# The filter rows of a long convolution at other distances in the DRAM scratch

## The chip, the cores and the metric

The kernel runs on one core of one Trainium2 chip. A core has a matrix engine (TensorE, PE in the profile), a vector engine (VectorE, DVE), a scalar engine (ScalarE, ACT), a general engine (GpSimd, POOL) and a sync engine (SyncE, SP) that here does nothing but issue DMA transfers. Sixteen DMA engines move data between DRAM and the on-chip memory SBUF. Matrix products land in a second on-chip memory, PSUM, of eight banks. Each engine runs its own list of instructions in order, and semaphores make one wait for another. The metric is the device time of one execution, in microseconds (us).

## The reference

Two independent computations are put side by side in the output, 512 columns each.

```python
def _A_ref(x, wqkv, wo):                      # attention: S = 2048, D = 512, 32 heads of 16
    qkv = transpose((x @ wqkv).reshape(B, S, 3, H, Dh), 2, 0, 3, 1, 4)
    q, k, v = qkv[0], qkv[1], qkv[2]
    scores = einsum("bhqd,bhkd->bhqk", q, k) * (Dh ** -0.5)
    p = softmax(scores, axis=-1)
    o = einsum("bhqk,bhkd->bhqd", p, v)
    return transpose(o, 0, 2, 1, 3).reshape(B, S, D) @ wo

def _B_ref(q, k, v, shift_k, ssm_k, ssm_D):   # gated long convolution, 512 channels
    k_shift = sum over t of k_pad[:, t:t + S, :] * shift_k[:, 3 - t]
    kv = k_shift * v
    y = causal convolution of kv with ssm_k along S   # written with FFTs
    y = y + kv * ssm_D
    return q * y

return concatenate([_A_ref(...), _B_ref(...)], axis=-1)
```

Inputs and output are bf16.

## The kernel before

Attention. The scores of 2048 queries by 2048 keys for 32 heads are made in blocks of 128 keys by 512 queries, and each block becomes one PSUM bank of 128x512. Two or three blocks form a chunk (T in the code). For each chunk TensorE makes the scores (line 791), ScalarE takes the exponentials of two banks at once (line 798, tile PT), VectorE and GpSimd take those of a third block by a polynomial (lines 817, 826, 827 and 290), and TensorE multiplies the results with the values (line 866). ScalarE thus has one instruction per chunk, 726 in all, each over 128x1024 elements.

Convolution. It runs on TensorE between the chunks, channel by channel, as products with Toeplitz matrices. For channel row d a tile of WR holds, in partition p, the 2048 filter values that begin p elements later than those of partition 0. One DMA per channel row builds it: its source is one row of the DRAM tensor `kz_scratch`, read 128 times, each time 2 bytes further (line 977). That is 128 reads of 4096 bytes out of one run of some 4.35 KB, 512 KB in all. WR has 14 such buffers (R_W = 14). Four channel rows are a quad, and the 64 small matmuls of a quad (line 998, in `conv_lags`) read their four buffers in turn. When a quad's last matmul has ended, four buffers are free, and SyncE issues the loads of the rows that lie 14 further on (`load_wr`, line 972, called from `conv_lags`). There are 512 such loads, in the order of d.

The scratch is written once, early. `kz_turn` (line 627) reverses the filter into KZS, a part of the WR buffers, with VectorE: partition p holds the four channels 4p to 4p+3, each as 2048 values and 128 zeros, 2176 elements or 4352 bytes. `kz_store` (line 632) adds the direct term ssm_D and issues four stores on SyncE's queue, one for each of the four channels of a partition. Each store takes one row of 4352 bytes from each of the 128 partitions. The rows are not stored in channel order: channel `chan(d)` lies in row d, so that the four channel rows of a quad are right for the four column strips of TensorE. In the scratch before, row d begins at byte 4352 d.

What stands behind the stores in SyncE's queue. `kz_store` is called together with `load_kv(5, ...)`: SyncE then issues the load of a piece of v (into QN) and of a piece of k (into QT), and GpSimd issues three more loads of k. VectorE multiplies these with the taps of the short filter (`kv_chunk`, lines 598, 602 and 618), pieces j = 7, 6, 5, ... 0 in that order, into KVP, the other operand of the convolution. When a piece is done, the loads of a later piece and some of the first loads of filter rows are issued, in the same queue of SyncE. The first 14 filter loads wait for all the stores (`h_kzw[0]`); later ones wait only for TensorE. The convolution begins when piece 0 is done (`start_conv`).

Order. The lists of PE, ACT, DVE and POOL are laid out beforehand by a planner in the kernel's code, which estimates when each operation ends (the class `Eng`, `Job` queues with due times). The planner takes 5600 ns for the four loads of a quad (DMA_NS), and SyncE's issues cost it nothing. The chip only runs the finished lists.

Of the kernel before, what the change touches and what calls it, by code (L numbers as in the profile page):

```python
# [7 lines left out]
BF16 = mybir.dt.bfloat16  # L8
# [4 lines left out]
S = 2048  # L13
# [11 lines left out]
C = 512  # L25
NB = S // 128
PAD = 128
LKZ = PAD + S
R_W = 14
R_PT = 5  # L30
R_O = 8
# [140 lines left out]
def bass_concat_heads__mha_block__ssm_conv_h3__prompt_kernel(  # L172
# [10 lines left out]
    out: bass.AP,  # L183
):
    x2, q2, k2, v2, out2 = A_x[0], B_q[0], B_k[0], B_v[0], out[0]
    kz_ap = nc.dram_tensor("kz_scratch", (C, LKZ), BF16).ap()

    ctxs = []

# [4 lines left out]
    def sem(name):  # L194
        return enter(nc.semaphore(name))

    def sb(name, shape, dt=BF16):
        return enter(nc.sbuf_tensor(name, shape, dt))
# [6 lines left out]
    PT = sb("PT", [128, R_PT, 3 * QB])  # L205
    WR = sb("WR", [128, R_W, S])
    KVP = sb("KVP", [128, 4 * NB + C * NB])
# [20 lines left out]
    def xn(t):  # L228
# [6 lines left out]
    wr_flat = WR[:, :, :].rearrange("p r w -> p (r w)")  # L235
    KZS = wr_flat[:, 0:4 * LKZ].rearrange("p (c m) -> p c m", c=4)
    DSS = wr_flat[:, 4 * LKZ:4 * LKZ + 4].rearrange("p (c m) -> p c m", m=1)
    o1 = 5 * S
# [10 lines left out]
    pe, act, dve, pool, sp = [Eng(sem(n), *k) for n, k in (("s_pe", (170.0,)), ("s_act", (100.0,)), ("s_dve", (-10.0, -85.0)),  # L249
                                                           ("s_pool", ()), ("s_sp", ()))]  # L250
# [93 lines left out]
    def dve_op(fn, deps=(), cost=692.0):  # L344
        return dve.op(fn, [force(d) for d in deps], cost=cost)
# [16 lines left out]
    def dma(eng, dsem, outp, inp, deps=(), transpose=False):  # L362
        h = dsem.add()

        def fn(e):
            f = e.dma_start_transpose if transpose else e.dma_start
            f(outp, inp).then_inc(dsem.sem, 16)  # L367
        eng.op(fn, deps, inc=False)
        return h
# [5 lines left out]
    d_tap, d_kz, d_kzw, d_wo = [DmaSem(sem(n)) for n in ("d_tap", "d_kz", "d_kzw", "d_wo")]  # L375
# [3 lines left out]
    d_outA = [DmaSem(sem(f"d_outA{i}")) for i in range(R_A)]  # L379
    d_wr = [DmaSem(sem(f"d_wr{i}")) for i in range(R_W)]  # L380

# [82 lines left out]
    h_kz0 = pool.op(lambda e: e.memset(KZS[:, :, S:S + PAD], 0.0))  # L464
# [127 lines left out]
    def kv_chunk(j):  # L592
        b = kvbuf[kv_buf[j]]
        st = {}

        def tap(m):
            in1 = TB[:, m:m + 1, :].broadcast_to([128, 2, D])
            st[m] = dve_job(lambda e: e.tensor_tensor(b[m], b[m], in1, ALU.mult),
                            [h_kv[(j, 0)], h_kv[(j, 1)], h_tb[m]], 750.0, 3000.0)

        def add(m):
            st["a"] = dve_job(lambda e: e.tensor_tensor(b[3], b[3], b[m], ALU.add), [st[m], st[3], st.get("a")], 750.0, 3500.0)

        def last():
            def then(h):
                h_kvfree[j] = h
                nxt = {4: 1, 3: None, 2: 0}.get(j, j - 3)
                if nxt is not None and nxt >= 0:
                    load_kv(nxt)
                for d in {6: (0, 1), 5: (2, 3), 4: (4, 11), 3: (8, 9, 12, 13), 1: (5, 6, 7)}.get(j, ()):  # L610
                    load_wr(d, [h])
                if j == 5:
                    load_qn(0, [h_kzt[0]], 4, NB)
                    line[0] += 5000.0
                elif j == 0:
                    start_conv(h)
            for i in range(2):
                dve_job(lambda e, i=i: e.tensor_tensor(KV[:, :, NB - 1 - 2 * j - i, :], quads(b[3][:, i, :]), quads(b[4][:, i, :]), ALU.mult),  # L618
                        [st["a"], h_xt[0]], 460.0, 4000.0 + i, then if i else None)
        return [lambda m=m: tap(m) for m in (3, 2)] + [lambda: add(2), lambda: tap(1), lambda: add(1),  # L620
                                                       lambda: tap(0), lambda: add(0), last]

    h_kzw = [None]
# [7 lines left out]

    def kz_store():
        h = dve_op(lambda e: e.tensor_tensor(KZS[:, :, S - 1:S], KZS[:, :, S - 1:S], DSS, ALU.add), [h_kzt[0]], 100.0)
        rows = kz_ap.rearrange("(o e h j) m -> o h e j m", e=2, h=2, j=2)
        for i in range(4):
            h_kzw[0] = dma(sp, d_kzw, rows[:, :, 1 - i % 2, i // 2, :], KZS[:, i, :], [h, h_kz0])

    kv_pieces += [lambda c=c: kz_turn(c) for c in range(4)] + [lambda: (kz_store(), load_kv(5, h_kzt[0]))]
    for j in range(7, -1, -1):
        kv_pieces += kv_chunk(j)  # L640
# [28 lines left out]
    def turn_first(cs, t0, dep):  # L669
        def fn(e):  # L670
            ins = None
            for c in cs:
                for t in range(t0, t0 + 2):
                    pbf = PS[:, first_bank[c], :].bitcast(BF16)
                    ins = e.transpose(pbf[:, 128 * t:128 * t + 128],
                                      xn(t)[:, 128 * c:128 * c + 128], IDN[:, :])
            return ins
        return pe_op(fn, [dep, h_idn], full(128, 2 * len(cs)))
# [3 lines left out]
    for c in range(4):  # L682
        h = turn_first([c], 2, h_xn[0])
        src = PS[:, first_bank[c], :].bitcast(BF16)[:, 0:512]
# [8 lines left out]
    def first_q(dc):  # L693
        return pe_op(lambda e: e.matmul(PS[:, 6, :], lhsT=WQ[:, dc, 0:128], rhs=xT[:, dc, 0:512],
                                        start=(dc == 0), stop=(dc == 3)), [h_x[0][dc], h_wq[0]], full(512, 1))

    def first_k(bank, c0, c1):
        def fn(e):
            ins = None
            for dc in range(4):  # L700
                ins = e.matmul(PS[:, bank, c0:c1], lhsT=WK[:, dc, 0:128], rhs=xT[:, dc, c0:c1],
                               start=(dc == 0), stop=(dc == 3))
            return ins
        return pe_op(fn, [*h_x[0], h_wk[0], bank_free[bank]], full(c1 - c0, 4))

    for dc in range(4):
        h = first_q(dc)
    evac_unit(("q", 0, 0), 6, h)
    h = first_k(7, 0, 128)
# [223 lines left out]
    def op_mm(qb, t, j0, j1, bank):  # L933
        dd = [bank_free[bank] if j0 == 0 else None, h_wop[0]]
        dd += [h_otn.get((4 * qb + j, t + 1), h_otn[4 * qb + j]) for j in range(j0, j1)]

        def fn(e):
            ins = None
            for j in range(j0, j1):
                ins = e.matmul(PS[:, bank, :], lhsT=OTN[:, (4 * qb + j) % R_O, t * 128:(t + 1) * 128], rhs=WOP[:, j, :],  # L940
                               start=(j == 0), stop=(j == 3))
            return ins
        return pe_op(fn, dd, full(512, j1 - j0))
# [28 lines left out]
    def load_wr(d, deps=()):  # L972
        r = d % R_W
        deps = [h_kzw[0], *deps] if d < R_W else [h_wrfree[d - R_W]]
        if d < R_W:
            line[0] += 1350.0
        src = bass.AP(tensor=kz_ap.tensor, offset=kz_ap[d, 0].offset, ap=[[1, 128], [1, S]])
        h_wr[d] = dma(sp, d_wr[r], WR[:, r, :], src, deps)

    def load_qn(i, deps, t0, t1):  # L980
# [3 lines left out]
    def conv_lags(qd, n0, n1):  # L984
# [6 lines left out]
        def fn(e):  # L991
            ins = None
            for n in range(n0, n1):
                for c in range(4):
# [4 lines left out]
                                   lhsT=KVP[:, o:o + 4 * (m * NB - n) - 3:4],  # L999
                                   rhs=WR[:, d % R_W, 128 * (NB - 1 - n):128 * (NB - n)],  # L1000
                                   start=(n == 0), stop=(n == NB - 1), tile_position=(0, 32 * c))
            return ins
        h = pe_op(fn, deps, [("col", c, 128) for n in range(n0, n1) for c in range(4)])
        if n1 == NB:
            for c in range(4):
                h_wrfree[4 * qd + c] = h
                if 4 * qd + c + R_W < C:
                    load_wr(4 * qd + c + R_W)
            if qd % 8 == 7:
                half = qd // 8 % 2  # L1010
                src = PS[:, BGB, :]
                src = bass.AP(tensor=src.tensor, offset=PS[:, BGB, 127:128].offset,
                              ap=[src.ap[0], [128, 4], [-1, 128]])
                bank_free[BGB] = dve_job(lambda e: e.tensor_copy(YB[:, half, :].rearrange("p (k i) -> p k i", k=4), src),
                                         [h, (lambda: h_yb.get(qd // 8 - 2, WAIT)) if qd >= 16 else None])
                h_yb_in[qd // 8] = bank_free[BGB]
# [39 lines left out]
    def start_conv(h):  # L1056
        h_kvc[0] = h
        state["started"] = True
        load_wr(10, [h])
        load_qn(0, [h], 0, 4)  # L1060
        now = at_of(h)
        state["dma"] = max(line[0], now) + 5000.0
        state["wr"] += [now - 1000.0, max(line[0], now) + 2000.0, state["dma"] - 1400.0]
        state["dma"] -= 1400.0
# [281 lines left out]
    for t in range(4):  # L1346
        h = op_mm(qb, t, 3, 4, tail_banks[t])
# [55 lines left out]
```

## Time and profile before

| | |
|---|---|
| Median of 3 runs | 846.76 us (844.92 to 847.79) |
| The profiled execution | 848.2 us, with a span of 846.4 us from its first to its last instruction |
| ScalarE (ACT) | busy 819.2 us, 97% |
| VectorE (DVE) | busy 798.4 us, 94% |
| TensorE (PE) | busy 719.9 us, 85%; granted clock 0.989 in the mean |
| GpSimd (POOL) | busy 290.6 us, 34% |
| DMA | 295.69 MB, 349 GB/s over the span |

How to read it. A row of the groups has line, engine, operation, out<-in tiles, shapes and count, then the busy time and the mean duration of one, then the idle time of the engine ahead of them and what ended most of it. "idle before <-X" says that X released the wait; "issue" is a wait for nothing that the profile shows. A row of stretches gives, for each window of the span, the busy time of each engine with the number of its instructions, the granted clock of TensorE, the mean busy share of the 16 DMA engines and what they moved per second. A row of the timeline gives a start, a duration (from the first start to the last end, where several are merged), engine, line, operation and count. SPq is SyncE's queue: the time shown there is that of issuing a transfer, not of moving the data, and "DMA to landing" is the time from the start of an issue until all of its data has arrived.

### The profile page before, as it was taken

What the parts mean: (1) busy time and instruction counts of PE and PEld (TensorE: products, weight loads), DVE (VectorE), ACT (ScalarE), POOL (GpSimd) and SP (SyncE); (2) the same over time, 40 slices, a digit from 0 to 9 for tenths busy, and PEclk for the clock granted to TensorE, in tenths of its full rate; (3) what the DMA queues carried; (4) which work ended last, traced back from release to release, by engine and by line L of the source; (5) the groups of instructions that cost most, each with busy time, mean ns of one, the idle gap of its engine ahead of it and who ended that gap; (6) DMA issues with size and microseconds to landing.
All of it is one profiled execution on the core that took longest, in us unless ns stands there. A gap on an engine that the chain in (4) does not pass through costs nothing.

```text
span 846.4 us, 29917 instructions
## 1 busy us (share of the span) xinstructions
PE 719.9 (85%) x13144; PEld 310.1 (37%) x13144; DVE 798.4 (94%) x1346; ACT 819.2 (97%) x732; POOL 290.6 (34%) x323
## 2 busy tenths in 40 slices
PE   8999888888888888888888888888888988888897
PEld 3322333433343343333333333333333343333332
DVE  3998899999999999999999899999999999999996
ACT  6998999999999999999999899999999999999997
POOL 3232233334333333333333433333332334333431
PEclk9999999999999999999999999999999999999999
DMA  9878699999999999999998999999999999999810
GB/s 325 302 266 291 219 405 351 382 407 406 387 351 389 387 408 382 386 359 389 386 381 303 374 365 407 366 409 377 359 343 363 374 411 384 380 395 387 342 51 26
DMA packets 88867, 295.69 MB, mean 349 GB/s; under 512 B 11173, under 2 KB 19362, under 8 KB 88482
## 3 DMA queue, kind: packets, MB, share of 16 engines
q1 hardware_dynamic: 82818, 280.00, 87.5%
q0 software_dynamic: 3776, 12.58, 4.2%
q8 instruction: 105, 1.72, 0.8%
q10 hardware_dynamic: 2144, 1.18, 0.5%
q14 instruction: 24, 0.20, 0.1%
HBM read 287.31 MB, written 6.42 MB: 347 GB/s over the span
## 4 chain that ended last, share of the span: by engine, by line
ACT 71%; PE 13%; DVE 12%; issue 2%; DMA 1%; POOL 1%; ACTq 0%; DVEq 0%
ACT PT L798 71%; PE PS L791 5%; PE PS L866 2%; DVE PTD L827 2%; DVE EM L826 2%; DVE EI L817 2%; PE PS L521 2%; DVE WKV L826 2%; PE PS L998 1%; PE PS L940 1%; DMA WKV<-in_A_wqkv_dram 1%; DVE OUTA L952 1%; PE PS L507 1%; PE PS L514 1%; DMA QT<-in_B_k_dram 1%
## 5 line engine op out<-in xcount | busy, mean ns | idle before, releaser
L798 ACT ACTIVATE PT<-PS 128x1024 bf16<-128x1024 f32 (+1 forms) x726 | 815.6, 1328 | 16.4 <-PE PS L791 14.8
L791 PE MATMUL PS<-QT,KTo 32*128 32x512 bf16 x2048 | 287.4, 387 | 113.3 <-ACT PT L798 92.8
L998 PE MATMUL PS<-WR,KVP 128*30 128x128 bf16 (+15 forms) x8192 | 258.7, 222 | 4.7 <-issue 4.2
L998 PEld LDWEIGHTS PS<-WR,KVP 128*29 128x29 bf16 (+15 forms) x8192 | 178.2, 95 | 79.7 <-issue 40.4
L290 POOL TENSOR_SCALAR EM<-EI 128x512 f32<-128x512 uint16 x131 | 126.9, 969 | 224.3 <-DVE WKV L826 114.8
L290 POOL TENSOR_SCALAR WKV<-EI 128x512 f32<-128x512 uint16 x130 | 125.9, 969 | 208.8 <-DVE EM L826 100.3
L866 PE MATMUL PS<-PT,VAF 128*32 128x512 bf16 x1787 | 188.6, 394 | 1.8 <-issue 0.7
L817 DVE TENSOR_SCALAR EI<-PS 128x512 int32<-128x512 f32 x261 | 177.3, 679 | 7.0 <-PE PS L791 6.7
L826 DVE SCALAR_TENSOR_TENSOR EM<-EM 128x512 f32<-128x512 f32 x262 | 175.0, 683 | 2.3 <-POOL EM L290 2.0
L826 DVE SCALAR_TENSOR_TENSOR WKV<-WKV 128x512 f32<-128x512 f32 x260 | 173.1, 682 | 2.0 <-POOL WKV L290 1.8
L791 PEld LDWEIGHTS PS<-QT,KTo 32*128 32x128 bf16 x2048 | 71.8, 91 | 275.3 <-ACT PT L798 218.2
L827 DVE SCALAR_TENSOR_TENSOR PTD<-EI,EM 128x512 uint16<-128x512 int32 x131 | 89.1, 681 | 0.4
L827 DVE SCALAR_TENSOR_TENSOR PTD<-EI,WKV 128x512 uint16<-128x512 int32 x130 | 88.2, 679 | 0.3
L866 PEld LDWEIGHTS PS<-PT,VAF 128*32 128x32 bf16 x1787 | 47.4, 93 | 109.1 <-issue 99.0
L866 PE MATMUL PS<-PTD,VAF 128*32 128x512 bf16 x261 | 79.2, 394 | 0.3
L1120 PE MATMUL PS<-IDN,ZER 128*32 128x512 bf16 x396 | 44.1, 382 | 0.0
L892 DVE STREAM_TRANSPOSE DT<-PS 128x512 f32<-128x512 f32 x31 | 22.1, 712 | 8.4 <-PE PS L866 8.2
L866 PEld LDWEIGHTS PS<-PTD,VAF 128*32 128x32 bf16 x261 | 19.8, 95 | 19.6 <-issue 8.1
L542 DVE TENSOR_TENSOR QT<-PS,MSK 128x1024 bf16<-128x1024 f32 x15 | 18.3, 1222 | 4.0 <-PE PS L507 3.9
L521 PE MATMUL PS<-WKV,xT 128*128 128x512 bf16 x64 | 19.2, 384 | 0.1
L367 POOL DMA_DIRECT2D out_dram<-OUTA x12 | 7.1, 593 | 34.8 <-DVE OUTA L952 34.8
L367 POOL DMA_DIRECT2D WR<-in_B_k_dram x15 | 11.0, 737 | 22.8 <-DVE KVP L618 14.8
(80 smaller groups left out, 295.2 us busy)
## 6 DMA issues: line engine op xcount, KB each, us to landing
WR<-kz_scratch SPq DMA_DIRECT2D x512, 512.0 KB, 8.0
WR<-in_B_k_dram POOLq DMA_DIRECT2D x15, 256.0 KB, 7.4
kz_scratch<-WR SPq DMA_DIRECT2D x4, 544.0 KB, 6.6
out_dram<-QN POOLq DMA_DIRECT2D x2, 1024.0 KB, 7.9
QT<-in_B_k_dram POOLq DMA_DIRECT2D x7, 256.0 KB, 6.2
out_dram<-OUTA POOLq DMA_DIRECT2D x12, 128.0 KB, 5.7
WR<-in_B_v_dram SPq DMA_DIRECT2D x5, 256.0 KB, 8.5
WR<-in_B_k_dram SPq DMA_DIRECT2D x5, 256.0 KB, 10.4
```

The costliest lines, as they stand in the source:

```text
L290: q.h = pool.op(lambda e: e.tensor_scalar(UB[m % len(UB)], f, PA, PB, ALU.mult, ALU.add), [h, fx.h, free], cost=Beside((h[0], h[1] + 1)))
L521: return e.matmul(PS[:, bank, :], lhsT=xT[:, dc, kt * 128:(kt + 1) * 128], rhs=WV[:, dc, :], start=(dc == 0), stop=(dc == 3))
L542: hh = dve_job(lambda e: e.tensor_tensor(QT[:, qb % 2, 2 * o:2 * o + 2, :], src, MSK[:, :, 0:1].broadcast_to([128, 2, QB]), ALU.mult), [h, ...
L791: ins = e.matmul(PS[:, bank, :], lhsT=KTo[32 * s:32 * s + 32, g // 2, kt * 128:(kt + 1) * 128], rhs=QT[32 * s:32 * s + 32, qb % 2, g, :], ...
L798: h_exp[T] = act.op(lambda e: e.activation(PT[:, T % R_PT, 0:n * QB], PS[:, banks[0]:banks[0] + n, :].rearrange("p b f -> p (b f)"), ACT.E ...
L817: h_fix[i] = job(lambda e: e.tensor_scalar(ei, PS[:, bank, :], FIX_LO, FIX_ADD, ALU.max, ALU.add), [h, h_pair.get(i - 4)], 692.0, end)
L826: js.append(job(lambda e, c=c: e.scalar_tensor_tensor(u, u, c, u, ALU.add, ALU.mult), [js[-1]], 693.0, due + 700.0 * (len(js) - 3)))
L827: js.append(job(lambda e: e.scalar_tensor_tensor(PTD[:, i % 4, :].bitcast(UINT16), ei, 2.0 ** -9, u, ALU.mult, ALU.add), [js[2], (lambda: ...
L866: ins = e.matmul(PS[32 * s:32 * s + 32, pvb(qb * NG + g), :], lhsT=VAF[:, kt, h * VW:h * VW + 32], rhs=rhs, start=first[b], stop=last[b], ...
L892: h_t = dve_job(lambda e: e.transpose(out=dt, in_=PS[:, pvb(n), :]), [h, h_mult.get(n - 2 if n == 2 else n - 1) if n != 1 else None], 717. ...
L998: ins = e.matmul(PS[32 * c:32 * c + m * NB - n, BGB, 128 * kk:128 * kk + 128], lhsT=KVP[:, o:o + 4 * (m * NB - n) - 3:4], rhs=WR[:, d % R_ ...
L1120: ins = e.matmul(PS[32 * s:32 * s + 32, pvb(n), :], lhsT=ZER[:, 0:32], rhs=IDN[:, :].rearrange("p (a f) -> p a f", a=1).broadcast_to([128, ...
```

## The change

The scratch becomes a flat tensor. Its 512 rows form four quarters of 128, and in each quarter the rows lie at another distance: 4480 bytes for rows 0 to 127, 5120 for 128 to 255, 6400 for 256 to 383 and 8448 for 384 to 511 (PITCH counts elements of 2 bytes). A list `kz_at` holds each row's first element. A row itself stays as it was, 2176 elements.

Since one store's rows no longer lie at one distance over the whole tensor, each of the four stores is cut into four, one for each quarter: 16 stores of 32 partitions in place of 4 of 128. Quarter g lies in partitions 32g to 32g+31. A load reads the same row as before, from its new place. In the lists of instructions, the four `kz_scratch<-WR` of SyncE become 16 at the same place; those of the other engines, and SyncE's other transfers and waits, stand in the same order as before.

```diff
+PITCH = (2240, 2560, 3200, 4224)
...
-    kz_ap = nc.dram_tensor("kz_scratch", (C, LKZ), BF16).ap()
+    kz_ap = nc.dram_tensor("kz_scratch", (C // 4 * sum(PITCH),), BF16).ap()
+    kz_at = [C // 4 * sum(PITCH[:d // 128]) + d % 128 * PITCH[d // 128] for d in range(C)]
...
         h = dve_op(lambda e: e.tensor_tensor(KZS[:, :, S - 1:S], KZS[:, :, S - 1:S], DSS, ALU.add), [h_kzt[0]], 100.0)
-        rows = kz_ap.rearrange("(o e h j) m -> o h e j m", e=2, h=2, j=2)
-        for i in range(4):
-            h_kzw[0] = dma(sp, d_kzw, rows[:, :, 1 - i % 2, i // 2, :], KZS[:, i, :], [h, h_kz0])
+        for g in range(4):
+            for i in range(4):
+                dst = bass.AP(tensor=kz_ap.tensor, offset=kz_at[128 * g + 4 * (1 - i % 2) + i // 2],
+                              ap=[[8 * PITCH[g], 16], [2 * PITCH[g], 2], [1, LKZ]])
+                h_kzw[0] = dma(sp, d_kzw, dst, KZS[32 * g:32 * g + 32, i, :], [h, h_kz0])
...
-        src = bass.AP(tensor=kz_ap.tensor, offset=kz_ap[d, 0].offset, ap=[[1, 128], [1, S]])
+        src = bass.AP(tensor=kz_ap.tensor, offset=kz_at[d], ap=[[1, 128], [1, S]])
```

## The prediction

> **What bounds the kernel now.** I read the page first: the busy times, then the chain of waits, then the groups on that chain and the DMA issues.
>
> ```profile
> span 846.4 us, 29917 instructions
> PE 719.9 (85%) x13144; PEld 310.1 (37%) x13144; DVE 798.4 (94%) x1346; ACT 819.2 (97%) x732; POOL 290.6 (34%) x323
> ...
> ACT 71%; PE 13%; DVE 12%; issue 2%; DMA 1%; POOL 1%; ACTq 0%; DVEq 0%
> ...
> L798 ACT ACTIVATE PT<-PS 128x1024 bf16<-128x1024 f32 (+1 forms) x726 | 815.6, 1328 | 16.4 <-PE PS L791 14.8
> ...
> L998 PE MATMUL PS<-WR,KVP 128*30 128x128 bf16 (+15 forms) x8192 | 258.7, 222 | 4.7 <-issue 4.2
> ...
> WR<-kz_scratch SPq DMA_DIRECT2D x512, 512.0 KB, 8.0
> ...
> kz_scratch<-WR SPq DMA_DIRECT2D x4, 544.0 KB, 6.6
> ```
>
> ScalarE sets the end: its 726 exponentials fill 815.6 of 846.4 us and stand idle for 16.4. DMA has 1% of the chain. The change touches two groups only, the 512 loads of filter rows and the four stores behind them, so the question is what either keeps waiting. The instructions of line 998 read the loaded rows; for them I asked who ended their waits, and for SyncE's queue what its issues wait for.
>
> ```profile
> L998 PE MATMUL PS<-WR,KVP x8192: 216/219/314, 90.9 to 812.8; 128*20 128x128 bf16 x9, 128*18 128x128 bf16 x9, 128*22 128x128 bf16 x8, 128*13 128x128 bf16 x8
> ...
>   issue: 44.6, 160
>   DVE YB L1014: 0.3, 1
> ```
>
> ```profile
> SPq L367 <- PE PS L998: 311.7, 86, 13.1
> ```
>
> No wait of line 998 was ended by a DMA. It is the other way round: SyncE waits 311.7 us for line 998 to free the buffers. How much time the data has in hand shows in one typical quad, number 100. Its last two loads were issued at 648.3 and 648.6 (first block: the issues, then their time to landing), its first matmul started at 658.92 (second block).
>
> ```profile
> L367 SPq DMA_DIRECT2D WR<-kz_scratch x2: 320/376/433, 648.3 to 648.6; - x2
> ...
> DMA to landing us min/median/max: 4.8/5.8/6.7
> ```
>
> ```profile
> 658.92 0.26 PE L998 MATMUL PS<-WR,KVP 128*32 128x128 bf16 x4
> ```
>
> The later one landed at 648.6 + 6.7 = 655.3, 3.6 us ahead of its use. That is the slack of the filter loads.
>
> It is a narrow one. The 128 quads take 812.8 - 90.9 = 721.9 us, 5.64 us each, and a quad needs 4 x 512 KB = 2.097 MB: the convolution asks for 372 GB/s. What the DMA engines can give shows where they were behind and worked without a gap, from 182 to 207.5 us:
>
> ```profile
> DMA  9999999999999999999999999999999999999999
> ...
> DMA packets 2826, 10.35 MB, mean 406 GB/s; under 512 B 313, under 2 KB 313, under 8 KB 2820
> ```
>
> At 406 GB/s a quad takes 5.17 us. So the reserve is 0.47 us per quad, 8% of the rate.
>
> **The change part by part.** The sum is made against the profiled execution: span 846.4, 848.2 us in all, so 1.8 us lie around the span. The median of the runs shown, 846.76, is 1.4 below it; I carry the difference over to the median.
>
> *1. The 512 loads from new places.* Number, size and order stay, and each still reads one run of some 4.35 KB 128 times, shifted by 2 bytes. Only the place of the next row differs. Before, 10.35 MB at 406 GB/s are some 20 consecutive rows, lying over 87 KB of the scratch at 4352 bytes, with no slice of that window under 90% busy; none of these places was slower than the others. I take 0 for this part. Upwards, the nearest rows are stretches in which the DMA engines gave less:
>
> ```profile
> 90.00:130.00 40.00, 33.90 (x707) 15.13 (x706) 36.62 (x61) 39.65 (x36) 14.66 (x15) 1.00 0.88 331
> ...
> 610.00:650.00 40.00, 33.08 (x676) 15.12 (x677) 37.46 (x64) 38.05 (x34) 12.68 (x14) 0.96 0.98 359
> ```
>
> These are no measured limits, but nothing nearer exists. At 359 GB/s a quad takes 5.84 us, 0.20 too long; over the 32 quads of a quarter 6.4 us, less 3.6 in hand, +2.8. At 331 it is 6.34 us, 0.70 too long, 22.4 less 3.6, +18.8. Downwards: all idle time of PE ahead of line 998 is 4.7 us, and if every part of it were hidden waiting for rows, faster loads could win no more: -4.7. I choose 0 because the window at 406 GB/s is the same operation at full load. What covers these loads is the 3.6 us and the 8%; when both are gone, line 998 waits in PE's list, behind it the next scores (line 791), and ScalarE behind those.
>
> *2. Sixteen issues for four.* SyncE's list around the stores:
>
> ```profile
> 26.60 4.00 SPq L367 DMA_DIRECT2D kz_scratch<-WR  x4
> 30.64 1.29 SPq L367 DMA_DIRECT2D QN<-in_B_v_dram  x1
> 31.98 1.58 SPq L367 DMA_DIRECT2D QT<-in_B_k_dram  x1
> 34.59 0.42 SPq L367 DMA_DIRECT2D WR<-in_B_v_dram  x1
> 35.05 0.58 SPq L367 DMA_DIRECT2D WR<-in_B_k_dram  x1
> 42.53 0.37 SPq L367 DMA_DIRECT2D WR<-in_B_v_dram  x1
> ...
> 43.46 0.94 SPq L367 DMA_DIRECT2D WR<-kz_scratch  x2
> ```
>
> Four issues took 4.00 us. An issue of 32 partitions is in no row. The lower bound is the shortest issue of a whole filter load above, 0.32 us: 16 x 0.32 = 5.1, 1.1 longer than now. The upper bound is the mean of today's stores, 1.0 us: 16.0, 12 longer. I take the 0.43 us of an unhindered filter load, the nearest kind: 6.9 us, +2.9. Queued behind are the v and k loads of piece 5, then those of piece 4. The k of piece 5 is needed first:
>
> ```profile
> DMA to landing us min/median/max: 7.6/7.6/7.6
> ```
>
> ```profile
> DMA to landing us min/median/max: 2.9/8.0/14.1
> ```
>
> ```profile
> 43.02 1.28 DVE L598 TENSOR_TENSOR QT<-QT,WR 128x1024 bf16<-128x1024 bf16 x2
> ```
>
> The first row is that load's time to landing, the second that of all transfers into or out of WR, the third the load's first use in VectorE's list. It was issued at 31.98, landed at 39.6 and was used at 43.02: 3.4 us in hand. They cover the +2.9 even if it were passed on whole. At +12 the load would be issued at 44 and land, with the shortest landing of 2.9 us, at 46.9: VectorE would stand 3.9 us. I count 0 here.
>
> *3. The stores' own transfer.* The bytes stay (4 x 544 KB = 2.23 MB), but each store now draws on 32 partitions. While the old stores ran, the DMA engines were full:
>
> ```profile
> 30.00:34.00 4.00, 4.00 (x36) 1.62 (x36) 3.96 (x8) 4.00 (x5) 0.00 (x0) 1.00 1.00 382
> ```
>
> At 382 GB/s the stores take 5.8 us. If 32 partitions give the same rate, this part costs 0; if a quarter of the partitions gave half of it, 5.8 us more, and the k of piece 5 would land at 45.4 instead of 39.6: VectorE stands 45.4 - 43.02 = 2.4 us. Of that the end can take all or nothing. The chain of waits in order of time says how it would get there:
>
> ```profile
> 73.05 0.43 DVE KVP L618
> 73.54 2.66 POOL QT L424
> 76.48 2.39 POOL QT L367 x4
> 78.88 4.35 DMA QT<-in_B_k_dram
> 83.25 0.69 DVE QT L598
> ```
>
> Here VectorE's work on the pieces is itself on the chain, up to the last piece's loads; a delay at 43 that is not made good by 73 arrives at the end. I take +0.5 for parts 2 and 3 together (bounds 0 and 3.9), nearer to 0, because the 3.4 us in hand are used up only when the stores take 5.8 + 3.4 = 9.2 us, at a rate under 241 GB/s.
>
> The Trainium skill speaks against that choice: "SBUF — State Buffer", section "Door 1: The DMA port swizzle", says that a transfer over 32 partitions reaches 8 of the 16 DMA ports, and gives 189 GB/s against 328 for 128 partitions. By these figures the stores would take, as an estimate, 10.1 us, the k of piece 5 would land at 43.9, and the sum would hold up to 0.9 instead of 0.5; no row here shows a 32-partition transfer.
>
> *4. The first filter loads wait for the stores.* They are issued from 43.46 on, when VectorE has freed the queue. The stores:
>
> ```profile
> L367 SPq DMA_DIRECT2D kz_scratch<-WR x4: 603/825/1617, 26.6 to 29.0; - x4
> ...
> DMA to landing us min/median/max: 4.7/6.6/8.2
> ```
>
> The last one landed at 29.0 + 8.2 = 37.2 at the latest. Delayed by 5.8 it lands at 43.0: nothing. The lists of the other engines are unchanged.
>
> Sum: 0 + 0 + 0.5 + 0 = +0.5; 848.7 in the profiled terms, **847.3 us** against the median of 846.76.
>
> **The rivals.**
>
> *A quarter of the rows is slow (slower).* One of the distances sets consecutive rows so that the DMA engines get less than 372 GB/s from them. Place: PE ahead of line 998, in one quarter of the time from 91 to 813 us. It decides from 8% loss on, after the 3.6 us are used up. Price +2.8 to +18.8, the middle +10: **857 us**. For it: the reserve is small, and the stretches above dip to 331. Against it: 406 GB/s over 20 rows at 4352 bytes. [...]
>
> *The stores from 32 partitions are half as fast.* Part 3 in full: VectorE stands 2.4 us ahead of 43 to 45 us and passes all of it on: **849.2 us**. For it: VectorE's pieces lie on the chain. Against it: between 43 and 73 us VectorE has idle time that may take it up:
>
> ```profile
> 53.00:63.00 10.00, 8.94 (x56) 2.25 (x54) 8.79 (x15) 9.95 (x12) 4.25 (x6) 1.00 0.92 301
> ```
>
> VectorE is busy 8.79 of 10 us there.
>
> *The loads get faster, and it counts.* Other distances lift the dips, and the 4.7 us ahead of line 998 fall away: **842.1 us**. Against it: with 3.6 us in hand nothing waits for the rows; a faster load waits longer in its buffer.
>
> *The change does nothing at all* is within my forecast: 846.8.
>
> **How the numbers follow.** About 0.3% (2.5 us) is what a measurement of this kernel can tell from no change: faster means below 844.2, slower above 849.3. Chances: forecast 0.50, a slow quarter 0.23, slow stores 0.17, faster loads 0.10. The forecast's own range is 845 to 849.3, with 0.03 of it above; slow stores fall 0.07 above, where the issues' upper bound adds to them. Slower: 0.23 + 0.07 + 0.03 = 0.33. Faster: 0.10. The same: 0.57. The range goes down to 844.0, leaving out most of the faster case, and up to 854, where half of the slow-quarter case, some 0.11, is left out.
>
> **What would show it.** Right: line 998 has no wait that a DMA ended, the filter loads land in 8.0 us in the median in all four quarters (used from 91 us on in steps of 180.5, issued some 20 us, 14 rows, ahead of that), the 16 stores are issued in about 7 us, and the first L598 on QT at 43 us has no idle time ahead of it. Slow stores: that L598 starts at 45 with a wait ended by a DMA. A slow quarter: landing times well over 8 us in one quarter with a DMA share at 1.00 and under 372 GB/s, and idle time ahead of L998. My forecast is wrong if ScalarE's idle time (16.4 us) grows by more than 2.5 us.

## The result, and the profile after

| | before | after |
|---|---|---|
| Median | 847.27 us (844.92 to 851.16, 4 runs) | 867.9 us (866.78 to 871.03, 4 runs) |
| Ratio of the times | | 1.0263, 95% interval 1.0231 to 1.0294 |
| Profiled execution | 848.2 us, span 846.4 us | 867.73 us, span 866.0 us |
| ScalarE busy, idle ahead of its exponentials | 819.2, 16.4 us | 821.3, 34.0 us |

The changed kernel is 2.6% slower, and the prediction of no change was wrong. (Two of the 24 executions behind e4_odd_shift below were slow ones of some 865 us and are left out of its medians; the one of them with a trace lost its time ahead of the convolution, which began at 104.8 instead of some 91 us, and had no wait of line 1002 for a load, so the loss shown here is another one.) In the code after, the line numbers have moved: 791 has become 795, 798 is 802, 998 is 1002, 367 is 369, 598 is 600. From the page of after, the span, the GB/s of 40 equal slices (each 21.65 us), the chain of waits, the two groups on it and the two groups of transfers that the change touches:

```profile
span 866.0 us, 29883 instructions
...
GB/s 326 273 284 287 227 399 360 386 406 402 362 383 386 392 408 364 401 372 398 379 387 291 362 411 385 382 402 365 337 317 318 344 344 334 346 354 342 351 66 25
...
ACT 50%; DVE 18%; DMA 16%; PE 11%; SPq 2%; issue 2%; POOL 1%; ACTq 0%; DVEq 0%
...
L802 ACT ACTIVATE PT<-PS 128x1024 bf16<-128x1024 f32 (+1 forms) x726 | 817.7, 1314 | 34.0 <-PE PS L795 32.0
...
L1002 PE MATMUL PS<-WR,KVP 128*30 128x128 bf16 (+15 forms) x8192 | 261.3, 224 | 22.8 <-DMA WR<-kz_scratch 20.0
...
WR<-kz_scratch SPq DMA_DIRECT2D x512, 512.0 KB, 8.6
...
kz_scratch<-WR SPq DMA_DIRECT2D x16, 136.0 KB, 3.8
```

DMA had 1% of the chain and now has 16%; ScalarE's share has fallen from 71% to 50%. The matmuls on the filter rows stood idle for 4.7 us, none of it for a DMA; now it is 22.8 us, 20.0 of them for the loads. ScalarE's idle time has grown by 17.6 us and its busy time by 2.1 us, together 19.7 against a span that is 19.6 us longer: nine tenths of the loss is ScalarE standing idle, nearly all of it for scores (line 795: 32.0 us where line 791 had 14.8), which stand behind line 1002 in PE's list.

Where in the span it happens, the GB/s row already tells: from the 29th slice on (606 us) only two slices reach 350, where most of the earlier ones are above 360. By stretches, with the columns that the prediction used (the last three are granted clock, DMA share, GB/s), first around that point:

```profile
570.00:610.00 40.00, 33.62 (x682) 14.97 (x687) 38.31 (x64) 38.87 (x34) 14.23 (x15) 0.96 1.02 375
610.00:650.00 40.00, 31.55 (x647) 14.14 (x640) 37.69 (x65) 38.27 (x34) 13.04 (x14) 1.00 1.01 326
```

The prediction placed the loads of a quarter 20 us ahead of a use in steps of 180.5 us from 91 us: the last quarter's loads, rows 384 to 511 at 8448 bytes, begin at about 612 us. There the DMA engines remain as busy as in the stretch ahead (1.01) and move 13% less. (The kernel before has a dip of its own in this stretch, to 359.) One stretch inside each quarter, after:

```profile
110.00:270.00 160.00, 135.40 (x2750) 62.09 (x2761) 157.03 (x264) 158.69 (x140) 56.48 (x62) 1.00 1.01 387
290.00:430.00 140.00, 115.02 (x2463) 53.45 (x2462) 138.58 (x236) 139.98 (x123) 51.19 (x52) 1.00 1.02 387
470.00:590.00 120.00, 99.65 (x2065) 45.74 (x2068) 116.67 (x196) 117.58 (x104) 42.92 (x44) 0.99 1.01 388
650.00:800.00 150.00, 118.40 (x2305) 52.27 (x2315) 129.38 (x216) 132.21 (x114) 47.04 (x50) 0.94 0.99 339
```

and the last of them before:

```profile
650.00:800.00 150.00, 126.12 (x2609) 57.15 (x2605) 147.18 (x249) 148.82 (x131) 54.53 (x58) 0.99 1.01 385
```

Three quarters move 387 to 388 GB/s; the fourth gets 339, where the convolution asks for 372 and the same stretch had 385. The time of a load from issue to landing (minimum, median, maximum) in the last quarter says the same; after:

```profile
DMA to landing us min/median/max: 8.8/13.9/18.2
```

before:

```profile
DMA to landing us min/median/max: 4.8/7.9/10.7
```

Loads that landed 3.6 us ahead of their use now take 6 us longer. The chain of waits in order of time, after (start, duration, what), shows what became of it:

```profile
689.85 5.06 ACT PT L802 x4
697.08 13.47 DMA WR<-kz_scratch
710.69 0.53 PE PS L1002 x24
...
714.45 16.67 DMA WR<-kz_scratch
731.26 0.66 PE PS L1002 x20
731.92 0.54 PE PS L795 x3
...
734.78 18.62 ACT PT L802 x16
...
759.49 13.27 DMA WR<-kz_scratch
```

Before, the chain from 689.66 us on was ScalarE's exponentials one after the other:

```profile
689.66 81.44 ACT PT L798 x71
```

Now loads stand on it again and again, with pieces of PE, VectorE and ScalarE between: of the chain from 690 to 830 us the loads are 51.3% and the exponentials 16.9%. The end of it, from the instructions of line 1002 (count, shortest, median and longest in ns, first and last start):

```profile
L1002 PE MATMUL PS<-WR,KVP x8192: 216/219/314, 91.7 to 832.4; 128*5 128x128 bf16 x9, 128*20 128x128 bf16 x9, 128*18 128x128 bf16 x9, 128*22 128x128 bf16 x8
```

The convolution takes 740.7 us instead of 721.9, +18.8, and starts 0.8 later; together that is the 19.6 of the span.

### The profile page after: what moved, and what is told of

Its sections match the earlier page's. It is cut to its first block, busy times and chain, and to the rows that moved or that the text cites. A ratio compares the mean times of both kernels' runs of the same rounds, so it can differ in the third digit from the quotient of the medians.

```text
span 866.0 us, 29883 instructions
## 1 busy us (share of the span) xinstructions
PE 720.5 (83%) x13098; PEld 310.7 (36%) x13144; DVE 799.7 (92%) x1346; ACT 821.3 (95%) x732; POOL 291.3 (34%) x323
## 4 chain that ended last, share of the span: by engine, by line
ACT 50%; DVE 18%; DMA 16%; PE 11%; SPq 2%; issue 2%; POOL 1%; ACTq 0%; DVEq 0%
ACT PT L802 50%; DMA WR<-kz_scratch 13%; PE PS L795 4%; DVE PTD L831 3%; DVE EI L821 3%; DVE EM L830 3%; DVE WKV L830 3%; SPq L369 2%; PE PS L870 2%; PE PS L1002 2%; DMA WR<-in_B_ssm_D_dram 2%; DMA QT<-in_B_k_dram 1%; DVE QT L544 1%; PE PS L509 1%; DVE DT L896 1%
## 5 line engine op out<-in xcount | busy, mean ns | idle before, releaser
L1002 PE MATMUL PS<-WR,KVP 128*30 128x128 bf16 (+15 forms) x8192 | 261.3, 224 | 22.8 <-DMA WR<-kz_scratch 20.0
L870 PEld LDWEIGHTS PS<-PTD,VAF 128*32 128x32 bf16 x261 | 19.8, 95 | 20.3 <-issue 9.0
```

What stands on the lines that cost most here:

```text
L870: ins = e.matmul(PS[32 * s:32 * s + 32, pvb(qb * NG + g), :], lhsT=VAF[:, kt, h * VW:h * VW + 32], rhs=rhs, start=first[b], stop=last[b], ...
L1002: ins = e.matmul(PS[32 * c:32 * c + m * NB - n, BGB, 128 * kk:128 * kk + 128], lhsT=KVP[:, o:o + 4 * (m * NB - n) - 3:4], rhs=WR[:, d % R_ ...
```

## The experiments

Two questions were open: is it the place of the rows and not the sixteen stores, and what about 8448 bytes is bad. The first kernel measures loads by themselves. Every time stands beside runs of the kernel before from the same chip; m1_rates and e1 to e3 ran on one chip, m2_rates, m3_rates, e4 and e5 on a second, m4_steps, e6 and e7 on a third, so rates of different kernels may also differ by the chip.

### Eight distances, loads alone (m1_rates)

```diff
+PITCH = (4352, 8448, 12544, 8192, 16640, 6400, 10240, 4352)
...
+            for s, p in enumerate(PITCH):
+                for d in range(N):
...
+                    src = bass.AP(tensor=rows[s].tensor, offset=d * p // 2, ap=[[1, 128], [1, S]])
+                    e.dma_start(WR[:, r, :], src).then_inc(d_wr[r], 16)
```

> All computation is left out: the kernel writes zeros to the output and then only loads filter-like rows, 64 at each of eight distances in turn, 14 loads in flight, nothing waiting for TensorE. The distances are, in this order, 4352, 8448, 12544, 8192, 16640, 6400, 10240 and again 4352 bytes. Theory A (what counts is the distance's remainder modulo 8192: consecutive rows that begin at nearly the same remainder crowd one part of the memory): 1.25 to 1.30 us per load at 4352, 12544 (the same remainder, 4352) and 6400; 1.5 to 1.6 us at 8448 and 16640 (both remainder 256) and as much or more at 8192 (remainder 0); 10240 (remainder 2048) in between. Theory B (a longer distance is slower as such): 4352 and 6400 at 1.27, 8448 at 1.55, and 12544 and 16640 at 1.55 or more. Theory C (the distance does not count; the last quarter is slow for another reason): 1.25 to 1.30 us at all.

Each distance has 64 loads of 512 KB, one distance after the other. The stretches in which only loads of one distance ran (columns here: window, length, DVE, POOL, clock, DMA share, GB/s), for 4352, 8448, 12544 and 8192:

```profile
115.00:180.00 65.00, 0.00 (x0) 0.00 (x0) 1.00 1.03 410
190.00:280.00 90.00, 0.00 (x0) 0.00 (x0) 1.00 0.96 330
295.00:360.00 65.00, 0.00 (x0) 0.00 (x0) 1.00 1.03 410
375.00:470.00 95.00, 0.00 (x0) 0.00 (x0) 1.00 1.01 313
```

16640 gave 359; 6400, 10240 and the second 4352 gave 410. For a load of 524,288 bytes, 410 GB/s are 1.28 us, 359 are 1.46, 330 are 1.59 and 313 are 1.68. A longer distance is not slower as such (12544 is as fast as 4352), and no other transfer runs beside these loads, so the slow rates need no other traffic. The remainder 2048 (10240), expected in between, was as fast as the rest. Slow are the distances that are a multiple of 8192 or 256 more.

### Sixteen stores, old distance (e1_all4352)

```diff
-PITCH = (2240, 2560, 3200, 4224)
+PITCH = (2176, 2176, 2176, 2176)
```

> The 16 stores of the changed kernel, but all rows 4352 bytes apart, as before the change. If the loss of 20 us lies in the distances (A and B): 847 us, within 0.3% of before (ratio 0.997 to 1.003), and no wait of line 1002 that a DMA ended. If the 16 smaller stores cost what I had allowed them: +0.5 to +2.4 us. If the last quarter is slow for another reason than distances (C): 866 us as in the changed kernel.

847.62 us (843.39 to 850.82, 10 runs) against 845.58 for the kernel before (15 runs); ratio 1.0017, interval 0.9989 to 1.0045. The row of the matmuls:

```profile
L1002 PE MATMUL PS<-WR,KVP 128*30 128x128 bf16 (+15 forms) x8192 | 259.4, 222 | 8.0 <-issue 6.7
```

The row names only what ended most of the 8.0 us; among the rest is a single wait for a load, of 0.5 us, where none was expected. Cutting the stores costs nothing that can be measured, though up to 0.45% (3.8 us) is inside the interval; the loss of 20 us comes with the distances.

### The slow quarter moved to the front (e2_first8448)

```diff
-PITCH = (2240, 2560, 3200, 4224)
+PITCH = (4224, 2560, 3200, 2240)
```

> The distances 8448 and 4480 bytes change places: 8448 in the first quarter, 4480 in the last. A and B: the stretch from 110 to 270 us moves about 335 GB/s with the DMA engines fully busy and line 1002 waits for DMAs there, the stretch from 650 to 800 us moves 375 to 390 GB/s with no such wait; in all some 862 to 870 us, since the slack is the same there. C: the last quarter stays slow, and the first stays at 370 to 400 GB/s.

875.52 us, one run. First and last quarter by stretches:

```profile
110.00:270.00 160.00, 129.84 (x2353) 55.68 (x2357) 134.02 (x223) 136.65 (x118) 47.27 (x49) 0.88 0.98 322
...
650.00:800.00 150.00, 126.60 (x2636) 57.88 (x2633) 147.38 (x248) 149.47 (x132) 53.23 (x57) 1.00 1.01 387
```

The slow stretch goes where the 8448 bytes go, and the last quarter, now at 4480, is as it was. So it is neither the end of the span nor the end of the tensor. The loss is 29.9 us, larger than expected: the rate in the first quarter is lower (322 against 339), and the granted clock is 0.88 against 0.94. Why the same distance costs more there isn't settled; the waits of line 1002 for loads are no longer in sum than in the changed kernel (19.8 us against 20.0).

### The last quarter at 12544 (e3_last12544)

```diff
-PITCH = (2240, 2560, 3200, 4224)
+PITCH = (2240, 2560, 3200, 6272)
```

> The last quarter at 12544 bytes instead of 8448. A (remainder 4352 modulo 8192, that of the kernel before): 847 us, ratio to before 0.997 to 1.004, no wait of line 1002 that a DMA ended. B (longer is slower): 866 us or more.

849.26 us (844.05 to 853.35, 6 runs) against 845.58; ratio 1.0044, interval 1.0009 to 1.0079. The last quarter:

```profile
650.00:800.00 150.00, 127.53 (x2617) 57.97 (x2614) 146.85 (x248) 148.54 (x131) 54.01 (x57) 0.98 1.01 385
```

Rows 4096 bytes further apart than in the changed kernel, and spread over half as much memory again, give 385 GB/s, and ScalarE's idle time is 16.3 us, as before. The distance as a length is not the cause. The ratio lies a little over what was expected; no wait for a row goes with it, and a loss of some 0.1 to 0.8% without a place in this profile stays unexplained.

### Remainders in small steps, loads alone (m2_rates, m3_rates)

```diff
-PITCH = (4352, 8448, 12544, 8192, 16640, 6400, 10240, 4352)
+PITCH = (0, 256, 8704, 9216, 9728, 4096, 7936, 16384)
```

> All computation is left out, as in m1_rates: 64 loads at each of eight distances, in this order: 0, 256, 8704, 9216, 9728, 4096, 7936 and 16384 bytes. Theory A in two forms. A1 (crowding: a part of the memory that serves one remainder modulo 8192 has too little throughput, whoever asks): at distance 0 every load reads the same row, so 0 and 256 are as slow as 8192 and 8448 were, 310 to 325 GB/s. A2 (conflict: what costs is that different places with the same remainder are read in turn): 0 and 256, where the loads read the same or adjoining bytes, run at 410 GB/s. Both: 7936 (256 below 8192) and 16384 (remainder 0) are slow, 310 to 352; 4096 is at 410; 8704, 9216 and 9728 (remainders 512, 1024, 1536) rise from about 325 to 410.

```diff
-PITCH = (4352, 8448, 12544, 8192, 16640, 6400, 10240, 4352)
+PITCH = (24832, 20736, 1024, 2048, 7168, 6144, 16896, 4352)
```

> All computation is left out, as in m1_rates: 64 loads at each of eight distances, in this order: 24832, 20736, 1024, 2048, 7168, 6144, 16896 and 4352 bytes. A: 24832 (remainder 256) and 16896 (512) are slow, 320 to 355 GB/s; 20736 (remainder 4352), 6144 (2048 below 8192) and 4352 run at 410; 7168 (1024 below 8192) like 9216 in m2_rates. A1: 1024 is like 9216, A2: 1024 and 2048 run at 410. B (a longer distance is slower): 20736, 24832 and 16896 are all slow.

The first two stretches of m2_rates, distances 0 (the same row, 64 times) and 256 (columns as in m1_rates):

```profile
115.00:205.00 90.00, 0.00 (x0) 0.00 (x0) 1.00 1.01 311
215.00:305.00 90.00, 0.00 (x0) 0.00 (x0) 1.00 0.87 331
```

All 24 stretches of the three kernels, sorted by how far the distance lies from a multiple of 8192 (the rates come from the same view):

| off a multiple of 8192 by | distance: GB/s |
|---|---|
| 0 | 0: 311, 8192: 313, 16384: 327 |
| 256 | 256: 331, 7936: 350, 8448: 330, 16640: 359, 24832: 337 |
| 512 | 8704: 397, 16896: 380 |
| 1024 | 1024: 406, 7168: 410, 9216: 410 |
| 1536 to 4096 | 2048, 4096, 4352 (twice in m1_rates, once in m3_rates), 6144, 6400, 9728, 10240, 12544, 20736: 410 each |

The rate goes by that remainder, within some 10%: 256 and 24832 bytes are as slow as 8448, and reading one row again and again, which touches 4.35 KB in all, is as slow as jumping 8192 bytes each time. A2 is out: 0 and 256 are slow. So it isn't rows far apart that are slow together, but rows that begin at the same or nearly the same place modulo 8192. The slow band is narrower than A had it: at 512 bytes off, 380 and 397 were measured where up to 355 had been expected, and from 1024 off on the loads alone have 406 to 410. That distance 0 and distance 8192 are slow for the same reason is likely from their like rates, not shown.

### Odd rows 4096 bytes further (e4_odd_shift)

```diff
-    kz_at = [C // 4 * sum(PITCH[:d // 128]) + d % 128 * PITCH[d // 128] for d in range(C)]
+    kz_at = [C // 4 * sum(PITCH[:d // 128]) + d % 128 * PITCH[d // 128] + (d // 384) * (d % 2) * 2048 for d in range(C)]
```

> As the changed kernel, the last quarter's rows at a mean distance of 8448 bytes, but each odd row 4096 bytes further on: an even row and the next odd one lie 12544 apart (remainder 4352), and the next even row 4352 behind that. A: consecutive rows no longer meet, 846 to 850 us, ratio to before 0.998 to 1.005, no wait of line 1002 that a DMA ended. If the mean distance or the place in the tensor is the cause: 866 us as in the changed kernel.

844.46 us against 844.42; ratio 1.0006, interval 0.9974 to 1.0037 (10 and 12 runs). The last quarter keeps its 8448 bytes on the average and its memory; only each second row is shifted by half of 8192. The whole loss is gone, and in its trace no wait of line 1002 was ended by a DMA. Rows two apart still lie at 16896, 512 off a multiple; that alone didn't slow the kernel.

### All quarters at 8448 (e5_all8448)

```diff
-PITCH = (2240, 2560, 3200, 4224)
+PITCH = (4224, 4224, 4224, 4224)
```

> All four quarters at 8448 bytes. If the loss is 128 loads at 335 GB/s per quarter in place of the 372 that the convolution asks for: about 20 us for the last quarter (after - before), 20 to 30 for each of the others, 925 to 950 us in all; ScalarE's idle time grows from 16 to about 100 us, with waits of line 1002 ended by DMAs from 110 us on. If another limit takes over (the planner's order lets the work ahead of the convolution run on): well under 925.

966.61 us, one run, 122.2 over the 844.42 of the kernel before; more than the 925 to 950 expected. Its waits for line 1002 (total, times, longest):

```profile
PE PS L1002 <- DMA WR<-kz_scratch: 97.3, 63, 3.4
```

The convolution takes 840.6 us (first start 90.6, last 931.2), 6.57 us per quad, so the loads get 2.097 MB / 6.57 us = 319 GB/s. The excess is the same open difference as in e2_first8448, and here too the granted clock is low, 0.88 to 0.95 over the four stretches.

### The step between partitions (m4_steps)

```diff
-PITCH = (4352, 8448, 12544, 8192, 16640, 6400, 10240, 4352)
+PITCH = (8192, 8192, 8192, 0, 0, 0, 8448, 8448)
+STEP = (1, 16, 128, 1, 16, 128, 16, 1)
...
-                    src = bass.AP(tensor=rows[s].tensor, offset=d * p // 2, ap=[[1, 128], [1, S]])
+                    src = bass.AP(tensor=rows[s].tensor, offset=d * p // 2, ap=[[STEP[s], 128], [1, S]])
```

> All computation is left out, as in m1_rates: 64 loads in each of eight settings. Now the step from one partition's read to the next changes too (2 bytes in the kernel). Distance of the rows / step, in this order: 8192/2, 8192/32, 8192/256, 0/2, 0/32, 0/256, 8448/32, 8448/2 bytes. A1 as crowding of many reads on the same few hundred bytes (modulo 8192) at one time: at a step of 2 the 128 reads of a load begin within 254 bytes, and 8192, 0 and 8448 run at 310 to 325 GB/s; at 32 they begin spread over 4 KB, at 256 over 32 KB, and all of these run at 405 to 410. If the rows' distance itself is what costs, whatever the reads within a load do: 8192 and 0 stay at 310 to 340 at every step.

The 128 reads of one load lie 2 bytes apart in the kernel; here also 32 and 256 bytes. For distance 8192, steps 2, 32 and 256:

```profile
110.00:205.00 95.00, 0.00 (x0) 0.00 (x0) 1.00 1.01 304
220.00:305.00 85.00, 0.00 (x0) 0.00 (x0) 1.00 1.01 334
325.00:390.00 65.00, 0.00 (x0) 0.00 (x0) 1.00 1.03 410
```

Distance 0 gave 295, 299 and 410; 8448 gave 350 at step 2 and 405 at step 32. So the distances 8192 and 0 are harmless once the 128 reads of a load begin spread over 32 KB (128 x 256): the slow case needs both, reads of a load that begin close together and loads that follow one another at nearly the same place modulo 8192. How close is not one figure: the step of 32 bytes (starts spread over 4 KB), expected to cure it, did so only at 8448 and left 8192 and 0 slow. Distances measured twice differ by up to 6% (8448: 330 and 350), so the slow rates are not exact figures.

### A remainder of 1024 and of 512 in the kernel (e6_last9216, e7_last8704)

```diff
-PITCH = (2240, 2560, 3200, 4224)
+PITCH = (2240, 2560, 3200, 4608)
```

> The last quarter at 9216 bytes, remainder 1024 modulo 8192, where the rows alone loaded at 410 GB/s. By that rate: 845 to 849 us, ratio to before 0.998 to 1.004, no wait of line 1002 that a DMA ended. If in the kernel, with other transfers beside, consecutive rows need more than 1 KB between their remainders: 850 to 866 us with such waits.

```diff
-PITCH = (2240, 2560, 3200, 4224)
+PITCH = (2240, 2560, 3200, 4352)
```

> The last quarter at 8704 bytes, remainder 512, where the rows alone loaded at 388 GB/s: 4 % above the 372 that the convolution asks for. By that rate no loss or a few us: 845 to 853 us, few waits of line 1002 that a DMA ended. If the rate in the kernel is lower than alone by as much as at 8448, or more: 855 to 866 us.

9216: 846.92 us (843.82 to 852.35, 10 runs) against 844.81; ratio 1.0023, interval 0.9993 to 1.0053, no wait for a row, 385 GB/s in the last quarter. 768 bytes more per row than in the changed kernel remove its loss. 8704, one run: 858.64 us, the second of the two cases of its expectation. Its last quarter:

```profile
650.00:800.00 150.00, 121.13 (x2454) 54.03 (x2456) 139.26 (x235) 141.87 (x124) 51.67 (x55) 0.98 1.00 361
```

and its waits:

```profile
PE PS L1002 <- DMA WR<-kz_scratch: 11.8, 13, 1.8
```

By themselves the loads at 8704 got 397 GB/s (388 in the mean with 16896, the other distance 512 bytes off), more than the 372 that are needed; in the kernel everything together got 361. Here a rate measured alone was too favourable. None of these versions beats the kernel before: no wait for a row was there to be removed.

## Why the prediction was wrong, point by point

**What bounds the kernel** was right: ScalarE, with a reserve of the filter loads of 3.6 us and 8%. The loss is what happens when that reserve is gone. By the prediction's own sign of being wrong, ScalarE's idle time was to grow by more than 2.5 us; it grew by 17.6.

**Part 1, 512 loads from new places, taken at 0, is the step that failed.** Its argument was the window at 406 GB/s: "some 20 consecutive rows, lying over 87 KB of the scratch at 4352 bytes", "none of these places was slower than the others". That covered twenty places and one relation between them, and it is the relation that the change alters. In its place the runs showed 339 GB/s in the last quarter, all transfers together, where the loads alone need 372, 20.0 us of waits for loads, and a convolution 18.8 us longer. m2_rates shows most plainly that it is not a matter of slow places: one place, with no new address at all, is slow at distance 0. The statement that the window "is the same operation at full load" held for a load by itself, not for the loads that are in flight together (WR has 14 buffers). That its upper bound, +18.8 from the stretch at 331 GB/s, equals the convolution's +18.8 is luck: that stretch is the start of the convolution, where the DMA engines were busy for 0.88 only, and no load stood at a bad distance.

**The rival of the slow quarter came true**, in its place (PE ahead of line 998, one quarter), with its signs (landing times well over 8 us, DMA share about 1.00, under 372 GB/s) and by its point of decision. Its price was mis-sized: +2.8 to +18.8, in the middle +10, against +20.6 in the medians (867.9 - 847.27) and 19.6 in the span. Put into the same formula, the measured 339 GB/s give 2.097 / 339 = 6.19 us per quad, 0.55 too long, times 32 less 3.6 = +13.9. That is too little because other transfers are in the 339: before, the DMA engines moved 385 in that stretch while the convolution asked for 372, so by this estimate 13 were others'. With 339 - 13 = 326 for the loads the formula gives 6.43 us per quad and +21.8. The measured value lies between; the prediction's formula left the others' share out. The case had been given a chance of 0.23, and the range that ended at 854 cut off the half of it that came.

The Trainium skill ("DMA: Bandwidth & Descriptors", "Latency and other measured facts") has a like pattern at much larger distances, and there between the partitions of one copy: 207 GB/s with rows 512 KiB apart, 103 with 4 MiB, 97 when 192 bytes are added to the 4 MiB and 214 when 4 KiB are. The trace agrees with the pattern for the distance between loads, far below that: 8192 bytes are slow (313 of 410 GB/s), 256 more don't cure it (330), and 4096 more do (410 at 12544). That the cause is the same is not shown.

**Part 2, sixteen issues**, was mis-sized: 0.43 us each, 6.9 in all. SyncE's list after (start, duration, transfer, count):

```profile
26.50 11.53 SPq L369 DMA_DIRECT2D kz_scratch<-WR  x16
38.07 0.59 SPq L369 DMA_DIRECT2D QN<-in_B_v_dram  x1
38.70 0.89 SPq L369 DMA_DIRECT2D QT<-in_B_k_dram  x1
```

They took 11.53 us, 0.72 each, between the bounds of 0.32 and 1.0. So the k of piece 5 was issued at 38.70 instead of 31.98, 6.7 later where 3.4 were in hand. VectorE's list shows the wait in brackets:

```profile
44.76 1.29 DVE L600 TENSOR_TENSOR QT<-QT,WR 128x1024 bf16<-128x1024 bf16 x2 [1.75 <-DMA QT<-in_B_k_dram]
```

It started 1.74 us later than the 43.02 of before; the prediction had counted this wait at 0. The convolution began 0.8 later (91.7 against 90.9), but how much of the 1.74 that is can't be told: with the same sixteen stores it began between 90.6 and 95.5 us in e1 to e3 and e5 to e7. The +0.5 for parts 2 and 3 is too small for these runs to confirm; e1_all4352 measures nothing at the end.

**Part 3, the transfer from 32 partitions.** The slow-stores rival expected a transfer of half the rate, and its sign came: the multiplication above began at 44.76, where the rival had 45, after a wait that a DMA ended. The issues alone account for it. The time from issue to landing of the first five stores after (issued 26.5 to 29.1) and of the next six (29.1 to 32.9):

```profile
DMA to landing us min/median/max: 3.3/4.3/4.6
```

```profile
DMA to landing us min/median/max: 2.8/3.4/4.3
```

The first five came 0.65 us apart, (29.1 - 26.5) / 4. At 139,264 bytes each, that is 214 GB/s, and the landing time did not grow: the transfers kept up with the issues. In e1_all4352 the sixteen issues took as long, 11.36 us, while the DMA engines were busy for only 0.70 between 34 and 38 us. So what was late was SyncE's issuing. That transfers from 32 partitions are slower themselves is not excluded: between 34 and 38 us the engines moved 238 GB/s at a share of 0.90 in the changed kernel and 367 at 1.02 before, though not for the same transfers. Nor is the rival's +2.4 at the end outside e1's interval. The Trainium skill ("SBUF — State Buffer", "Door 1: The DMA port swizzle") gives 189 GB/s for one transfer of 1 MiB over 32 partitions and about 218 as the limit of their eight ports. The 214 lie between the two and speak against neither; a faster issue was not tried.

**Part 4**, the first filter loads wait for the stores: nothing, as predicted.

**Open.** Why 8448 bytes cost 20 us in the last quarter, 30 in the first and 122 in all four; what part the lower granted clock has in that (0.94 in the changed kernel's slow quarter, 0.88 in that of e2_first8448, 0.88 to 0.95 in e5_all8448, but 0.98 in that of e7_last8704, the same as in e3_last12544 without a wait for a load; no run changed the clock by itself); and what in the memory makes 8192 bytes the period. That reads on one spot stand in line there would fit m4_steps, and is not shown.

## What to carry to other kernels

When a change moves where data lies, check the relation between transfers that are in flight together, not only the size and shape of one: here consecutive loads within 512 bytes of a multiple of 8192 of each other got 295 to 397 GB/s where others got 406 to 410. First ask what reserve the stage has: with 8% in hand, loads that are 20% slower alone (330 of 410 GB/s) went through to the end, and 768 more bytes of distance (9216) gave the time back. If a measurement at full load is taken as proof that a part costs nothing, name what it held constant; that is what the change may alter.

## What had not been expected of the hardware

- Reading the same 4.35 KB again and again is slow: 311 GB/s at distance 0 against 410 at 4352, while the DMA engines' share is 1.01 and 1.03: they are as busy and move less.
- The period of 8192 bytes, for loads alone with full rate from 1024 bytes off a multiple on (406 to 410) and a cure by a step of 256 bytes between the partitions (410 at distances 0 and 8192).
- The granted clock of TensorE was lower in most quarters in which PE waited for rows: 0.94 in the changed kernel's last quarter, 0.88 in the first quarter of e2_first8448, 0.99 to 1.00 in the other quarters of both; but 0.98 in the slow quarter of e7_last8704.
- A small store occupies SyncE almost as long as a large one: 0.72 us for 136 KB from 32 partitions, 1.0 us for 544 KB from 128.
